# A state-space convolution with a gated top-2 feed-forward: the forward transform evicts its even part and then the full sum, the mirrored part is summed by an accumulating DMA, and the x term moves to TensorE

## The chip, the cores and the metric

The kernel runs on one core of a Trainium2 chip. The metric is device time in microseconds (us), lower is better. Engines: PE is TensorE (matmul), DVE is VectorE, ACT is ScalarE, POOL is GpSimd, and SP issues most of the DMAs. PSUM is the memory that PE writes its sums to (eight banks); SBUF holds everything else.

## The reference, cut to what matters

x is `A_u`, 2048 x 512 in bfloat16: 2048 time steps, 512 channels.

```
def _A_ref(u, A_re, A_im, B_re, B_im, C_re, C_im, log_dt, Dskip):
    dt = jnp.exp(log_dt)[:, None]
...
    P = jnp.exp(logdA[:, :, None] * l[None, None, :])
    K = jnp.einsum("dn,dnl,dn->dl", Cc, P, dB).real
...
    Yf = Uf * Kf[None, :, :, :]
    y = irfft2(Yf, (1, L2)).astype(jnp.bfloat16)[:, :, 0, :L]
    return y.transpose(0, 2, 1) + u * Dskip[None, None, :]

g = _sigmoid((x * gate_w).sum(-1, keepdims=True))
a = _A_ref(x, ...)
b = _B_ref(x, ...)    # x, plus a feed-forward's result on the 2 rows with the largest x @ w_r
return g * a + (1 - g) * b
```

So a is a causal convolution of each channel with a kernel K of 2048 taps, itself a sum over 128 complex exponentials per channel; b is x with two rows corrected; the output mixes them by a gate for each time step.

## The kernel before, in words

The program is recorded first: every step is an entry of one list (`Prog.op`), with the buffers that it reads and writes. The text `ORDER` then gives the order in which these entries stand on each engine, `SECOND` says which of two possible engines takes an entry that could run on either, and `PLACES` gives the PSUM bank or buffer of each short-lived tile (`Prog.fixed`). `Prog.emit` works out the semaphore waits. Nothing is reordered at run time: each engine takes its list from the front, and an instruction that waits holds back all that stand behind it. Costs that are written with the entries serve a planner outside the kernel.

One-line helpers record single steps, so many instructions have a helper's line: L452 `TT` (DVE tensor_tensor), L456 and L457 `TS`, L459 `STT`, L463 `AC` (an ACT activation), L465/L467 `EV` (a copy, by ACT or DVE), L469/L471 `SQ` (a square, either engine), L475/L477 `SCL` (a multiplication by a constant, either engine), L480 `DMA`.

The work, in the order of recording:

- `exps1`, `exps2` (lines about 600): powers of the exponentials, by small matmuls with scaled identities (L598, L609) and ACT exponentials.
- `routing`: transposes of x (L767), the gate and the router's scores (L782), the two rows with the largest score (L797, L801), and their feed-forward (L850, L864). The result is scattered into the output's memory, into which x has been copied, and x is reloaded from there into its buffer `U` by `reload()`.
- `tab1`, `tab2`: tables of sines and products for the two column halves h = 0, 1 of 256 channels (ACT: int32 to sine and the masks, L463, L668, L696; DVE: products).
- `forward(blk)` for the two blocks of 1024 time steps (L902): a transform to frequencies with the constants `F`, whose time steps are split into even and odd ones. For each of four frequency tiles `ft` and each of two parts (real, imaginary) 8 matmuls of 128x512 sum even and odd steps in a bank; the sum is evicted to `X` (pm = 0). Then 4 matmuls with `UO`, minus twice the odd steps, go on top, and even minus odd is evicted as the mirrored part (pm = 1). `UO` is made by one 128x2048 scaling.
- `kgen(h)` (L920): K's samples from the tables, evicted to `KA`, and picked from there by L933, L937, L946, L949 into `KC`.
- `kspec(h)` (L975): the spectrum `KK` of K, by matmuls of 128x256. Its second half starts from the first: as a carry by PE matmuls of 128x512 (L967) for the halves h listed in `CPE`, else by an ACT activation into PSUM (L962, shown under L463).
- `products(h, qds, blks)`: products of `X` and `KK` as DVE multiplications of 128x4096, for the second block with an accumulating DMA issued by POOL (L1019, 1 MB) that adds one product to another, and sums and differences of 128x1024 (all L452) that write the result over `X`.
- `inverse(h)` (L1052): the inverse transform with the constants `G` (2 MB, loaded late). Each PSUM tile is first filled with the x term, x times a factor for its time steps, by ACT (L1037, two activations of 128x256, shown under L463); a one-hot matmul (L1040) adds to the rows that the feed-forward changed; 16 matmuls of 128x256 add the transform; two evictions (L1060, ACT or DVE) multiply by the gate. Output DMAs of 128 KB follow.

What the change and the prediction's steps touch: `forward`, `products`, `inverse`, `kspec` through `CPE`, the end of `routing` (the factor of the x term), `late`, the buffers, and the orders. The factor of the x term and the gate stand in columns of a small tile:

```
TS(SG(0, 128, 64, (1, 16)), SGB(0, 128, 32, (1, 16)), 1.0e-20, ALU.max, ...)
P.op(DVE, lambda h: h.reciprocal(SG(0, 128, 80, (1, 16)), SG(0, 128, 64, (1, 16))), ...)
TT(SG(0, 128, 96, (1, 16)), SG(0, 128, 80, (1, 16)), SGB(0, 128, 48, (1, 16)), MUL, ...)
```

## Time and profile before

| what | value |
|---|---|
| runs | 154.81, 155.19, 155.6 us (median 155.19) |
| profiled execution | 155.34 us, of which the span from first to last instruction is 153.5 us |
| granted TensorE clock, mean | 0.989 |
| instructions in the span | 3887 |
| matmuls of the forward transform (L902) | 192, 44.7 us busy |
| matmuls of the inverse (L1052) | 256, 29.1 us busy |
| x term on ACT (L463, 128x256 into PSUM) | 32, 14.3 us busy |
| accumulating DMAs (L1019) | 4 of 1 MB, 7.9 to 11.6 us from issue to landing |
| DMA traffic | 26.21 MB, mean 171 GB/s |

A line of the profile names the code line, the engine, the operation, where it writes and reads (`AR` is the SBUF arena, `ps` is PSUM), and the shape. "Busy" adds the time in which such instructions ran; neighbours on one engine overlap at their edges, so a mean duration can be longer than the step from one to the next. "Idle before" is the engine's idle time just ahead of them, and what ended it. The chain of work is followed backwards from the last instruction, at each step to what released it. Most of the kernel has DVE and PE running side by side, so the chain's shares say which of the two it happened to follow, and the windows say whether the other was idle.

### The profile page before, as it was taken

Reading aid. Unit: us, or ns where it says so; the run is one execution under the profiler, and the core shown is the slowest. Engines: PE = TensorE matmul, PEld = TensorE weight load, DVE = VectorE, ACT = ScalarE, POOL = GpSimd, SP = SyncE. Lnnn points to the kernel's source line nnn. Section 1 sums busy time; section 2 is a strip of 40 time slices with the busy share of each in tenths; the row PEclk is TensorE's granted clock in tenths of the full one; section 3 lists DMA queues with packets and bytes.
Section 4 is the critical chain, followed back from the end, with each engine's and each line's share of the span. In section 5 each row is a group of like instructions: output and inputs, shape, how many; then the busy total and the mean of one; then the engine's idle time right before and its main releaser. Section 6 shows DMA issues by size and latency. Waiting matters only on the chain.

```text
span 153.5 us, 3887 instructions
## 1 busy us (share of the span) xinstructions
PE 138.1 (90%) x1661; PEld 100.0 (65%) x1661; DVE 137.3 (89%) x207; ACT 124.4 (81%) x206; POOL 9.7 (6%) x17
## 2 busy tenths in 40 slices
PE   1877999999999999999989999988866999999990
PEld 1666734665446444996447879985754888887870
DVE  0599999999999999899999999992999999999941
ACT  3399899989979999999958968576599599995530
POOL 3000000000100000014000000340000001130000
PEclk9999999995999999999999999999999999999999
DMA  4899999937700001700079200199998000799974
GB/s 138 255 341 411 409 404 398 352 102 277 275 0 4 0 0 26 242 14 1 0 190 384 114 4 0 33 184 190 229 391 345 11 2 4 136 173 188 249 214 138
DMA packets 13523, 26.21 MB, mean 171 GB/s; under 512 B 1175, under 2 KB 8098, under 8 KB 13346
## 3 DMA queue, kind: packets, MB, share of 16 engines
q1 hardware_dynamic: 11410, 21.11, 39.1%
q0 software_dynamic: 1120, 4.20, 15.6%
q10 hardware_dynamic: 976, 0.66, 1.4%
q8 instruction: 13, 0.21, 0.6%
q14 instruction: 4, 0.03, 0.1%
HBM read 19.66 MB, written 4.20 MB: 155 GB/s over the span
## 4 chain that ended last, share of the span: by engine, by line
DVE 47%; PE 36%; DMA 9%; ACT 3%; issue 3%; SPq 1%
DVE AR L452 39%; PE ps L902 18%; PE ps L1052 7%; DMA AR<-AR 7%; PE ps L920 6%; DVE AR L467 3%; PE ps L850 2%; DMA AR<-in_A_log_dt_dram 2%; DVE AR L477 2%; ACT AR L463 1%; PE ps L598 1%; DVE AR L456 1%; DVE AR L459 1%; PE ps L864 1%; DVE AR L797 1%
## 5 line engine op out<-in xcount | busy, mean ns | idle before, releaser
L452 DVE TENSOR_TENSOR AR<-AR 128x1024 bf16<-128x1024 bf16 (+10 forms) x127 | 110.6, 923 | 7.8 <-ACT AR L463 5.4
L467 ACT ACTIVATE AR<-ps 128x1024 bf16<-128x1024 f32 (+10 forms) x57 | 48.2, 865 | 14.1 <-PE ps L975 4.7
L902 PE MATMUL ps<-AR 128*128 128x512 bf16 x192 | 44.7, 388 | 0.0
L902 PEld LDWEIGHTS ps<-AR 128*128 128x128 bf16 x192 | 18.8, 101 | 21.4 <-issue 1.9
L1052 PE MATMUL ps<-AR 128*128 128x256 bf16 x256 | 29.1, 273 | 1.8 <-DMA AR<-c_inv 1.4
L1052 PEld LDWEIGHTS ps<-AR 128*128 128x128 bf16 x256 | 24.7, 98 | 5.5 <-DVE AR L452 2.7
L975 PE MATMUL ps<-AR 128*128 128x256 bf16 x160 | 19.3, 273 | 1.5 <-ACT AR L467 0.7
L463 ACT ACTIVATE AR<-AR 128x1024 bf16<-128x1024 int16 (+5 forms) x24 | 18.3, 774 | 1.7 <-DMA AR<-in_A_log_dt_dram 1.2
L975 PEld LDWEIGHTS ps<-AR 128*128 128x128 bf16 x160 | 15.3, 98 | 5.4 <-ACT AR L467 1.8
L463 ACT ACTIVATE ps<-AR 128x256 f32<-128x256 bf16 (+1 forms) x36 | 18.2, 544 | 0.1
L920 PEld LDWEIGHTS ps<-AR 128*128 128x128 bf16 x512 | 17.9, 96 | 0.7 <-ACT AR L696 0.4
L920 PE MATMUL ps<-AR 128*128 128x84 bf16 (+1 forms) x512 | 18.1, 196 | 0.0
L1060 ACT ACTIVATE AR<-ps,AR 128x256 bf16<-128x256 f32 x26 | 11.8, 478 | 5.7 <-PE ps L1052 5.6
L463 ACT ACTIVATE AR<-ps 128x512 bf16<-128x512 f32 (+1 forms) x18 | 12.1, 789 | 1.9 <-PE ps L598 1.9
L477 ACT ACTIVATE AR<-AR 128x256 int32<-128x256 f32 (+2 forms) x25 | 12.4, 528 | 0.0
L668 ACT ACTIVATE AR<-AR 128x1024 int32<-128x1024 int32 (+1 forms) x10 | 8.9, 888 | 0.1
L1019 POOL DMA_DIRECT2D AR<-AR x4 | 4.9, 1216 | 60.4 <-DVE AR L452 30.6
L477 DVE TENSOR_SCALAR AR<-AR 128x256 int32<-128x256 f32 (+3 forms) x25 | 8.4, 350 | 0.0
L767 PE MATMUL ps<-AR 128*128 128x128 bf16 x64 | 4.4, 220 | 1.8 <-DVE AR L452 1.2
L767 PEld LDWEIGHTS ps<-AR 128*128 128x128 bf16 x64 | 3.6, 98 | 2.6 <-DVE AR L452 1.4
L933 PE MATMUL ps<-AR 128*32 128x128 bf16 x64 | 4.7, 421 | 0.6 <-ACT AR L467 0.6
L609 PE MATMUL ps<-AR 128*128 128x128 bf16 x8 | 2.0, 475 | 3.1 <-DMA AR<-in_A_C_im_dram 3.1
(63 smaller groups left out, 81.8 us busy)
## 6 DMA issues: line engine op xcount, KB each, us to landing
AR<-AR POOLq DMA_DIRECT2D x4, 1024.0 KB, 9.2
AR<-c_ksp SPq DMA_DIRECT2D x5, 512.0 KB, 4.3
AR<-in_A_u_dram SPq DMA_DIRECT2D x4, 512.0 KB, 7.3
AR<-c_fwd SPq DMA_DIRECT2D x4, 512.0 KB, 10.2
AR<-out_dram SPq DMA_DIRECT2D x4, 512.0 KB, 8.2
AR<-c_inv SPq DMA_DIRECT2D x1, 2048.0 KB, 14.6
AR<-in_B_w_up_dram SPq DMA_DIRECT2D x1, 1792.0 KB, 11.6
AR<-in_B_w_gate_dram SPq DMA_DIRECT2D x1, 1792.0 KB, 17.0
```

The lines of the kernel that those rows point to most:

```text
L452: return P.op(DVE, lambda h: h.tensor_tensor(out=o, in0=a, in1=b, op=op), rd, wr, cost=cst or tt_cost(o, a, b), **k)
L463: return P.op(ACT, lambda h: h.activation(out=o, in_=a, func=func, scale=scale, bias=bias), rd, wr, cost=0.185 + nel(o) * 0.833e-3 + (0.09 ...
L467: return P.op((ACT, DVE), (lambda h: h.activation(out=o, in_=a, func=ACTF.Copy), lambda h: h.tensor_copy(o, a)), rd, wr, cost=(0.185 + n * ...
L477: return P.op((ACT, DVE), (lambda h: h.activation(out=o, in_=a, func=ACTF.Copy, scale=c), lambda h: h.tensor_scalar(out=o, in0=a, scalar1= ...
L668: P.op((DVE, ACT), (lambda hh: hh.tensor_scalar(out=w, in0=w, scalar1=16384.0, scalar2=None, op0=ALU.add), lambda hh: hh.activation(out=w, ...
L767: last = h.transpose(bb(0, 128, db * 256 + t_ * 128, (1, 128)), U(0, 128, (2 * q + t_) * D + db * 128, (1, 128)), IDN(0, (1, 128)))
L902: last = h.matmul(o, w, x, start=(pm + par + st == 0), stop=(par == 1 and st == 3), skip_group_check=(pm == 1))
L920: last = hh.matmul(pb(0, 128, g // 6 * 512 + g % 6 * W4 + o, (1, n)), TP[h][1 - i // 2](0, 128, (b0 + g) * 128, (1, 128)), r[i](0, 128, (b ...
L975: last = hh.matmul(pb(0, 128, n * 256, (1, 256)), KP[u](0, 128, tau * 128, (1, 128)), KC[h](0, 128, jg * 256, (1, 256)), start=(k == 0 and ...
L1019: P.op(POOL, lambda hh, p=p, t=t: hh.dma_start(v(p), v(t), accum_op=ADD, max_dma_last_dim=4096), qk(t, 0, 1, 2, 3), qk(p, 0, 1, 2, 3), cos ...
L1052: r = hh.matmul(pb(0, 128, e * 256, (1, 256)), G(0, 128, ((par * 2 + part) * 4 + ft) * 512 + (2 * t2 + e) * 128, (1, 128)), X(0, 128, h * ...
L1060: P.op((ACT, DVE), (lambda hh, o=o, i_=i_, g_=g_: hh.activation(out=o, in_=i_, func=ACTF.Copy, scale=g_), lambda hh, o=o, i_=i_, g_=g_: hh ...
```

## The change

The forward transform now sums the 4 matmuls of the even steps first and evicts them, multiplied by -2, to the mirrored part (pm = 1); the 4 matmuls of the odd steps go on top, and the full sum is evicted to pm = 0. `UO` and its scaling are gone, and each part takes 8 matmuls where it took 12. For every pair of frequency tiles and each block POOL issues one accumulating DMA (512 KB, four in all) that adds pm = 0 to pm = 1: odd minus even, so the last sum and difference of `products` change places.

The x term is a matmul: `late` makes 16 identities of 128x128, each multiplied by the factor of one tile of time steps (rounded to bfloat16), by ACT activations, and two matmuls of 128x256 per PSUM tile start the inverse. Seven operations of 16 elements (of which two are copies) work out the rounded factor and a gate that makes up for the rounding. `CPE` takes in h = 1, so the carry of the second spectrum is on PE. The evictions of the inverse stand two to an entry, on ACT or as one DVE tensor_tensor, except at the very end.

`X` is laid out by blocks, the feed-forward's buffers move with it, and `ORDER`, `SECOND` and `PLACES` are new. With them the first DMA on SP is log_dt, the loads of `F`, the feed-forward's weights and the smaller inputs stand in another order, three reloads of `U` instead of two stand ahead of `G` and one behind it, and ACT has four table loads instead of two. `kgen`, `tab1`, `tab2` and the rest of `kspec` compute what they did.

```diff
@@ -253,7 +253,7 @@
 NM = len(MAG2)
 ACC = ()
 DAC = ((0, 0), (0, 1), (1, 0), (1, 1))
-CPE = (0,)
+CPE = (0, 1)
 GROUPS = [[2 + 4 * i + k for k in range(4)] for i in range(4)] + [[1, 18, 19, 20]]
 KUSE = [(0, 0), (0, 1), (0, 2), (0, 3), (1, 4)]
 NU = len(KUSE)
@@ -369,29 +369,29 @@
...
@@ -496,11 +496,10 @@
-        UO = B("uo", oF + 16 * KB, 4 * KB)
-        XB = [[B("x%d%d" % (h_, k_), oX + (16 * h_ + 8 * k_) * KB, 8 * KB) for k_ in range(2)] for h_ in range(2)]
+        XB = [[B("x%d%d" % (h_, k_), oX + (16 * k_ + 8 * h_) * KB, 8 * KB) for k_ in range(2)] for h_ in range(2)]
@@ -518,8 +517,8 @@
-        XT = [B("xt%d" % i, oX + (16 * (i // 2) + 8 + 4 * (i % 2)) * KB, 4 * KB) for i in range(4)]
-        WD = [B("wd%d" % i, oX + (16 * i + 8) * KB, 8 * KB) for i in range(2)]
+        XT = [B("xt%d" % i, oX + (16 + 4 * i) * KB, 4 * KB) for i in range(4)]
+        WD = [B("wd%d" % i, oX + (16 + 8 * i) * KB, 8 * KB) for i in range(2)]
@@ -545,6 +544,7 @@
+        DX16 = B("dx16", oI + 16 * KB, 4 * KB)
@@ -791,6 +791,13 @@
+            EV(SGB(0, 128, 64, (1, 16)), SG(0, 128, 96, (1, 16)), [(SG, "x")], [(SGB, "x")])
+            EV(SG(0, 128, 0, (1, 16)), SGB(0, 128, 64, (1, 16)), [(SGB, "x")], [(SG, "xr")])
+            TT(SG(0, 128, 32, (1, 16)), SG(0, 128, 96, (1, 16)), SG(0, 128, 0, (1, 16)), SUB, [(SG, "x"), (SG, "xr")], [(SG, "d")])
+            TS(SG(0, 128, 48, (1, 16)), SG(0, 128, 0, (1, 16)), 1.0e-30, ALU.max, [(SG, "xr")], [(SG, "r")])
+            P.op(DVE, lambda h: h.reciprocal(SG(0, 128, 48, (1, 16)), SG(0, 128, 48, (1, 16))), [], [(SG, "r")], cost=0.3)
+            TT(SG(0, 128, 32, (1, 16)), SG(0, 128, 32, (1, 16)), SG(0, 128, 48, (1, 16)), MUL, [(SG, "r")], [(SG, "d")])
+            STT(SG(0, 128, 112, (1, 16)), SG(0, 128, 32, (1, 16)), 1.0, SG(0, 128, 64, (1, 16)), ADD, MUL, [(SG, "d"), (SG, "m")], [(SG, "n")])
@@ -881,29 +888,37 @@
         def late():
             P.op(POOL, lambda h: h.memset(OHR(0, 128, 0, (1, len(ERT) * 128)), 0.0), [], [OHR], cost=0.4)
             DMA([(OHR(32, NE, 0, (1, len(ERT) * 128)), oh_c[:, :])], [], [(OHR, "e")], NE * 1024)
+            for j in (1, 0):
+                def da(hh, j=j):
+                    for i in range(8 * j, 8 * j + 8):
+                        r = hh.activation(out=DX16(0, 128, i * 128, (1, 128)), in_=CB(0, 128, 0, (1, 128)), func=ACTF.Copy, scale=SG(0, 128, 0 + i, (1, 1)))
+                    return r
+                P.op((DVE, ACT), (lambda hh, j=j: hh.tensor_tensor(out=DX16(0, 128, j * 1024, (128, 8), (1, 128)), in0=CB(0, 128, 0, (0, 8), (1, 128)), in1=SGB(0, 128, 64 + 8 * j, (1, 8), (0, 128)), op=MUL), da),
+                     [CBI, (SGB, "x"), (SG, "xr")], [(DX16, j)], cost=(1.22, 2.9))
         def reload():
             for j in (1, 0):
                 for k in range(2):
                     DQ([(U(0, 128, (j * 8 + k * 4) * D, (2 * D, 2), (1, 2 * D)), dr(out, (1024 * j + 512 * k) * D, (2 * D, 128), (256 * D, 2), (1, 2 * D)))], [DX], [(U, (t, h_)) for t in range(8 * j + 4 * k, 8 * j + 4 * k + 4) for h_ in range(2)], 524288)
 
         def forward(blk):
-                SCL(UO(0, 128, 0, (1, 4 * D)), U(0, 128, (blk * 8 + 1) * D, (2 * D, 4), (1, D)), -2.0, uk(*range(blk * 8 + 1, blk * 8 + 8, 2)), [UO])
                 for ft in range(4):
                     pb = psum(2, full=True)
-                    for pm in range(2):
+                    for par in range(2):
                         for part in range(2):
-                            def fw(h, blk=blk, ft=ft, pm=pm, pb=pb, part=part):
+                            def fw(h, blk=blk, ft=ft, par=par, pb=pb, part=part):
                                 last = None
-                                o = pb(0, 128, part * 512, (1, 512))
-                                for par in range(pm, 2):
-                                    for st in range(4):
-                                        w = F[ft](0, 128, ((par * 4 + st) * 2 + part) * 128, (1, 128))
-                                        x = UO(0, 128, st * D, (1, D)) if pm else U(0, 128, (blk * 8 + st * 2 + par) * D, (1, D))
-                                        last = h.matmul(o, w, x, start=(pm + par + st == 0), stop=(par == 1 and st == 3), skip_group_check=(pm == 1))
+                                for st in range(4):
+                                    last = h.matmul(pb(0, 128, part * 512, (1, 512)), F[ft](0, 128, ((par * 4 + st) * 2 + part) * 128, (1, 128)), U(0, 128, (blk * 8 + st * 2 + par) * D, (1, D)),
+                                                    start=(par + st == 0), stop=(st == 3), skip_group_check=(par == 1))
                                 return last
-                            P.op(PE, fw, [F[ft]] + ([UO] if pm else uk(*range(blk * 8, blk * 8 + 8))), [(pb, part)], cost=(8 - 4 * pm) * 0.2157)
-                        EV(X(0, 128, blk * 4096 + ft // 2 * 1024 + pm * 512 + ft % 2 * 256, (2048, 2), (8192, 2), (1, 256)), pb(0, 128, 0, (512, 2), (256, 2), (1, 256)),
-                           [pb], [xk(hh, blk, part, pm, ft) for hh in range(2) for part in range(2)])
+                            P.op(PE, fw, [F[ft]] + uk(*range(blk * 8 + par, blk * 8 + 8, 2)), [(pb, part)], cost=4 * 0.2157)
+                        o, i_, sc = X(0, 128, blk * 8192 + ft // 2 * 1024 + (1 - par) * 512 + ft % 2 * 256, (2048, 2), (4096, 2), (1, 256)), pb(0, 128, 0, (512, 2), (256, 2), (1, 256)), (-2.0, 1.0)[par]
+                        P.op((ACT, DVE), (lambda hh, o=o, i_=i_, sc=sc: hh.activation(out=o, in_=i_, func=ACTF.Copy, scale=sc), lambda hh, o=o, i_=i_, sc=sc: hh.tensor_scalar(out=o, in0=i_, scalar1=sc, scalar2=None, op0=ALU.mult)),
+                             [pb], [xk(hh, blk, part, 1 - par, ft) for hh in range(2) for part in range(2)], cost=(0.185 + 1024 * 0.833e-3, 0.16 + 1024 * 1.04e-3))
+                    if ft % 2:
+                        xv = lambda pm: X(0, 128, blk * 8192 + ft // 2 * 1024 + pm * 512, (2048, 4), (1, 512))
+                        xs_ = lambda pm: [xk(hh, blk, part, pm, f) for hh in range(2) for part in range(2) for f in (ft - 1, ft)]
+                        P.op(POOL, lambda hh, d=xv(1), c=xv(0): hh.dma_start(d, c, accum_op=ADD), xs_(0), xs_(1), cost=1.3, nbytes=524288, dma=True, tag="acc")
 
         def kgen(h):
             r = RW[h]
@@ -1024,7 +1039,7 @@
                 for parts in (((0,), (1,)) if last(h, blk, qds[-1]) else ((0, 1),)):
                     n, p0 = len(parts), parts[0]
                     y = lambda pm: p(0, 128, (2 * p0 + pm) * W, (2 * W, n), (1, W))
-                    for pm, op in ((0, ADD), (1, SUB)):
+                    for pm, op in ((0, SUB), (1, ADD)):
                         TT(X(0, 128, xo(blk, p0, pm), (2048, n), (1, W)), y(0), y(1), op, qk(p, *parts), [xk(h, blk, part, pm, ft) for part in parts for ft in fts])
         def inverse(h):
             for blk in (1, 0):
@@ -1032,9 +1047,12 @@
                 tbs = lambda t2, par: [blk * 8 + (2 * t2 + e) * 2 + par for e in range(2)]
                 for t2 in range(2):
                     for par in range(2):
-                        pb = bufs[t2, par] = psum(seed=True)
-                        for e, tb in enumerate(tbs(t2, par)):
-                            AC(pb(0, 128, e * 256, (1, 256)), U(0, 128, tb * D + h * HC, (1, HC)), ACTF.Copy, [(SG, "x"), (U, (tb, h))], [(pb, e)], scale=SG(0, 128, 96 + tb, (1, 1)))
+                        pb = bufs[t2, par] = psum(full=True)
+                        def xt(hh, pb=pb, tbs_=tbs(t2, par)):
+                            for e, tb in enumerate(tbs_):
+                                r = hh.matmul(pb(0, 128, e * 256, (1, 256)), DX16(0, 128, tb * 128, (1, 128)), U(0, 128, tb * D + h * HC, (1, HC)), start=(e == 0), stop=False, skip_group_check=True)
+                            return r
+                        P.op(PE, xt, [(DX16, blk)] + [(U, (tb, h)) for tb in tbs(t2, par)], [pb], cost=2 * 0.1092)
                         for e, tb in enumerate(tbs(t2, par)):
                             if tb in ERT:
                                 P.op(PE, lambda hh, pb=pb, e=e, tb=tb: hh.matmul(pb(0, 128, e * 256, (1, 256)), OHR(0, 128, ERT.index(tb) * 128, (1, 128)), ZB(0, 128, h * HC, (1, HC)), start=False, stop=False, skip_group_check=True),
@@ -1050,15 +1068,22 @@
                                         for c in cs:
                                             part, ft = c % 2, 2 * q + c // 2
                                             r = hh.matmul(pb(0, 128, e * 256, (1, 256)), G(0, 128, ((par * 2 + part) * 4 + ft) * 512 + (2 * t2 + e) * 128, (1, 128)),
-                                                          X(0, 128, h * 8192 + blk * 4096 + part * 2048 + ft // 2 * 1024 + par * 512 + ft % 2 * 256, (1, 256)), start=False, stop=(q == 1 and e == 1 and c == 3), skip_group_check=True)
+                                                          X(0, 128, blk * 8192 + h * 4096 + part * 2048 + ft // 2 * 1024 + par * 512 + ft % 2 * 256, (1, 256)), start=False, stop=(q == 1 and e == 1 and c == 3), skip_group_check=True)
                                     return r
                                 P.op(PE, iv, [G] + [xk(h, blk, part, par, ft) for part in sorted({c % 2 for c in cs}) for ft in (2 * q, 2 * q + 1)], [pb.buf], cost=2 * len(cs) * 0.1092)
                             if q == 0:
                                 continue
-                            for e, tb in enumerate(tbs(t2, par)):
-                                o, i_, g_ = U(0, 128, tb * D + h * HC, (1, HC)), pb(0, 128, e * 256, (1, HC)), SG(0, 128, 64 + tb, (1, 1))
-                                P.op((ACT, DVE), (lambda hh, o=o, i_=i_, g_=g_: hh.activation(out=o, in_=i_, func=ACTF.Copy, scale=g_), lambda hh, o=o, i_=i_, g_=g_: hh.tensor_scalar(out=o, in0=i_, scalar1=g_, scalar2=None, op0=MUL)),
-                                     [pb.buf, (SG, "m")], [(U, (tb, h)), (pb.buf, "r")], cost=(0.473, 0.484))
+                            tb0 = tbs(t2, par)[0]
+                            for ee in (((0,), (1,)) if last(h, blk, q) else ((0, 1),)):
+                                def oa(hh, ee=ee, pb=pb, tb0=tb0):
+                                    for e in ee:
+                                        tb = tb0 + 2 * e
+                                        r = hh.activation(out=U(0, 128, tb * D + h * HC, (1, HC)), in_=pb(0, 128, e * 256, (1, HC)), func=ACTF.Copy, scale=SG(0, 128, 112 + tb, (1, 1)))
+                                    return r
+                                def od(hh, ee=ee, pb=pb, tb0=tb0):
+                                    e, n, tb = ee[0], len(ee), tb0 + 2 * ee[0]
+                                    return hh.tensor_tensor(out=U(0, 128, tb * D + h * HC, (2 * D, n), (1, HC)), in0=pb(0, 128, e * 256, (256, n), (1, HC)), in1=SG(0, 128, 112 + tb, (2, n), (0, HC)), op=MUL)
+                                P.op((ACT, DVE), (oa, od), [pb.buf, (SG, "n")], [(U, (tb0 + 2 * e, h)) for e in ee] + [(pb.buf, "r")], cost=((0.473, 0.484) if len(ee) == 1 else (0.88, 0.7)))
                 for st in range(4):
                     tb = blk * 8 + st * 2
                     DMA([(dr(out, (1024 * blk + 256 * st) * D + h * HC, (2 * D, 128), (D, 2), (1, HC)), U(0, 128, tb * D + h * HC, (D, 2), (1, HC)))],
```

More of the change, by code (lines that the diff above doesn't have):

```diff
@@ L389 @@
[L389 to L391 removed]
+    "000000000000000000000000000000000000100000000000000000000000000010100010101010100000100100010000000000000000000000000000010001000000000000000000000011"
@@ L769, in routing @@
                 P.op(PE, tr, uk(2 * q, 2 * q + 1) + [CBI], [bb], cost=0.455)
-                EV(XT[0](0, 128, q * 256, (8 * KB, 2), (L, 2), (1, 256)), bb(0, 128, 0, (512, 2), (256, 2), (1, 256)), [bb], [(XT[i], q) for i in range(4)])
+                EV(XT[0](0, 128, q * 256, (2 * L, 2), (L, 2), (1, 256)), bb(0, 128, 0, (512, 2), (256, 2), (1, 256)), [bb], [(XT[i], q) for i in range(4)])
             w8 = misc(True)
@@ L985, in products @@
             q0 = qds[0] * 1024
-            xo = lambda blk, part, pm: h * 8192 + blk * 4096 + part * 2048 + pm * 512 + q0
+            xo = lambda blk, part, pm: blk * 8192 + h * 4096 + part * 2048 + pm * 512 + q0
             fts = [2 * qd + e for qd in qds for e in range(2)]
```

45 lines of the change are left out of this document (22 added, 23 removed).

## The prediction

> **What bounds the kernel.** I read the busy shares first, then the chain that ended last, then the rows behind its last half, and the windows of its stages.
>
> The page, first and fourth part:
>
> ```profile
> PE 138.1 (90%) x1661; PEld 100.0 (65%) x1661; DVE 137.3 (89%) x207; ACT 124.4 (81%) x206; POOL 9.7 (6%) x17
> ...
> DVE 47%; PE 36%; DMA 9%; ACT 3%; issue 3%; SPq 1%
> ```
>
> Three engines are over 80% busy. Taking work from one of them gains only where that one is late. The chain (start, us, what) from the first product on:
>
> ```profile
> 92.74 4.48 DVE AR L452 x2
> 97.23 0.10 DVE AR L474
> 97.32 0.22 issue
> 97.54 10.16 DMA AR<-AR
> 107.70 0.02 issue
> 107.72 11.17 DVE AR L452 x14
> 118.90 0.47 issue
> 119.36 1.94 DVE AR L452 x4
> ...
> 138.71 10.83 PE ps L1052 x96
> 149.54 0.02 issue
> 149.56 0.48 ACT AR L1060
> 150.04 0.02 issue
> 150.07 0.48 DVE AR L1060
> ```
>
> From the first 4096-wide product at 92.74 a fixed sequence follows: two products, an accumulating DMA of 10.16 us, 11.17 us of DVE sums, then the inverse transform. The windows (span, then busy us and count of PE, PEld, DVE, ACT, POOL) say who limits it:
>
> ```profile
> 20.00:30.00 10.00, 9.76 (x79) 4.58 (x77) 9.90 (x31) 9.97 (x12) 0.00 (x0) 1.00 1.05 384
> 60.00:70.00 10.00, 10.00 (x235) 8.57 (x234) 9.40 (x16) 9.97 (x15) 1.32 (x2) 1.00 0.36 108
> 119.30:150.50 31.20, 29.86 (x269) 25.91 (x269) 28.64 (x35) 23.44 (x54) 2.40 (x2) 1.00 0.58 125
> ```
>
> Ahead of the products PE, DVE and ACT are all full. From the first inverse matmul (119.30) to the last (149.54) PE ran 269 matmuls in 30.24 us with 0.37 us of gaps: 0.111 us each. The end is PE-bound. The rows that the change touches (busy, mean ns, idle before):
>
> ```profile
> L902 PE MATMUL ps<-AR 128*128 128x512 bf16 x192 | 44.7, 388 | 0.0
> L463 ACT ACTIVATE ps<-AR 128x256 f32<-128x256 bf16 x32 | 14.3, 483 | 0.0
> L463 ACT ACTIVATE ps<-AR 128x1024 f32<-128x1024 bf16 x4 | 4.1, 1026 | 0.1
> ```
>
> **The sum, part by part.** It is made against the profiled execution: span 153.5 and 1.84 us around it, 155.34; the median of the runs is 155.19, so I correct nothing.
>
> *Forward transform.* 64 of 192 matmuls go. In the chain 40 of them take 8.74 us, 0.2185 each: PE is relieved of 14.0 us, nearly all between 32.7 and 74.7, where the chain is PE. But DVE and ACT are full beside it, so I ask what each needs up to the first product.
>
> DVE: two 1024-wide products less (2 x 0.60 by the chain), two 1024-wide scalings less (2 x 0.34), the 2048-wide scaling for the old -2 x odd buffer less (0.6), three 256-wide more (3 x 0.20), a 512-wide less (0.2), a reciprocal more (0.25): -1.8. The waits behind L696, L463 and L463 (0.6, 0.28, 0.31) go, since what they waited for now stands earlier: -1.2. At the start log_dt is loaded first (-0.55), but the copy of the constants no longer fills DVE's wait for PE L598 (0.85 becomes 1.95): +0.55. DVE alone could begin the first product at 92.74 - 2.4 = 90.3.
>
> PE and ACT: kernel generation (L920, 256 matmuls, 8.9 us) starts at about 59.8, when both its inputs and the first half of the forward are done, against 61.4. Then 32 forward matmuls (7.0), the extraction (about 4), four spectra of 16 at 0.111 (7.1); ACT's sixth spectrum eviction, which the second product needs, ends at about 91.2. A load of the spectrum's first constants now follows the last forward matmul (4.3 us to landing) and may add 0.5 to 0.8. So the first product starts at 91.2 to 92.4; I take 91.9, which is 0.8 earlier.
>
> *Four accumulating DMAs on POOL.* The rows have four of twice the size (L1019: issue 1.2 us, landing 7.9 to 11.6). At half the size I take 1.2 and 5. The last has its inputs by about 74 and stands behind a memset that waits for ACT at about 82; it lands near 88, while the sums that read its target come after 107. At nothing, then, with some 17 us of cover; below nothing only by the evictions, whose count is unchanged. The swapped ADD and SUB cost nothing.
>
> *Carry of the second spectrum on PE.* Four ACT seeds of 1.03 go (row above); eight 512-wide matmuls come, 1.7 us on PE, 0.44 of it behind the first inverse matmul.
>
> *x term.* 32 ACT seeds (14.3 us) go; 32 PE matmuls of 0.111 come (3.6), 8 ahead of the first inverse matmul and 24 behind it. Sixteen 128x128 activations come: nearest rows 171 ns (128x8) and 394 (128x256), so 2.7 to 6.3 us; I take 4. They stand in the 15 us while the first accumulating DMA runs, and the spectrum evictions behind them finish 3 us before DVE reads them. The seven 16-element operations (0.16 to 0.3 us each) stand in DVE's wait for that DMA (1.8 us before).
>
> *Table loads.* Two become four. Each is 1.28 us (20.47 to 21.75), and the next activation began at 21.77: +2.6. With two 1024-wide squares moved to ACT (+2.1) and one scaling and other steps off it, ACT has 3.3 us more ahead of the products. It idles there at 74.5 to 90.7 for 4.2 us in sum, which hides it if nothing DVE needs sooner is delayed. The page "ScalarE: Activation LUTs" of the Trainium skill (section "What ACT_TABLE_LOAD costs") gives 1283 ns for the load, which the row shows, and about 1380 ns for a drain on top, which the 0.02 us gap does not show; by that rule two more would be +5.3.
>
> *From the first product on.* The first accumulating DMA lands 14.9 us after it, as before (92.74 to 107.7); then DVE has two 4096-wide products moved behind that wait (2 x 2.24), nine 1024-wide steps (9 x 0.56) and 0.6 of small ones: 10.1. First inverse matmul at 91.9 + 25.0 = 116.9, against 119.30. The inverse constants, then waited for (landing 14.6 us after issue at 104.55), are issued a little sooner with one reload less ahead; about 116.5, a near tie.
>
> *The end.* From there PE has 256 + 24 + 8 one-hot + 4 spectrum matmuls, 292 x 0.111, and 0.44 of carry: 32.85 us against 30.24. Last matmul 149.75; two evictions 0.95 and the output DMA 2.95 as before: span 153.7, with the 1.84 around it 155.5. A span up to 154.2 (first product at 92.4) gives 156.0. I take **155.8**: the 2.4 us that the first half gains are paid back by PE's 2.6 us at the end, where ACT's relief is worth nothing. DVE's last sum, at 146.4 before, comes 2.5 us earlier and is not the end either.
>
> **The rivals.**
>
> *Faster, 153.2.* The first accumulating DMA took 10.16 us while others shared the queues; the shortest took 7.9. If it gets that, DVE's wait shrinks by 2.3 us, and with the first product at 91.2 or sooner the inverse can start 2.6 us earlier than in the forecast, if its constants are in by 114.3. For it: one reload less, and 391 GB/s in the slices where they came. Against: they came just when needed before.
>
> *Slower, 158.4.* ACT takes the bound: between 10 and 70 us it idles under 0.9 in 10, and the sines that DVE multiplies come through it. If the two loads delay the tables, DVE waits 2.6 us and the first product starts at 94.5. It decides when kernel generation's inputs come later than about 60.5. By the Trainium skill's drain rule, named above, another 2.7 would follow: 161.1; the 0.02 us gap speaks against it.
>
> *POOL's DMAs are late, 158.* The sums of the first half need the halved target; if an accumulating DMA waits while DVE is busy, all that follows slides by some 2.2 us (12.4 instead of 10.2 to landing). The four rows of L1019 speak against it: issues of 1.19 to 1.26 us beside a DVE busy 10 of 10. The Trainium skill's page "SBUF — State Buffer" (section "SBUF: two separate sides") says that POOL cannot write descriptors while DVE runs a two-port mode; the rows show no such stall.
>
> *The change does not do what it says:* the counts of the order do show 128 forward matmuls and no seeds, so I give it nothing.
>
> **How the numbers follow.** Forecast (154.9 to 156.6) 0.38; faster 0.28 (151.8 to 154.4); slower by ACT 0.26 (156.6 to 160); the drain rule 0.03; late POOL DMAs 0.05. No change means within 0.5%, about what a measurement of this kernel can tell: 154.4 to 156.0. Of the forecast 0.22 fall inside and 0.16 above. So faster 0.28, same 0.22, slower 0.50. The range reaches into both neighbours and leaves about 0.05 below and 0.12 above: 152.4 to 159.0; the forecast's own range stands above.
>
> **What would show it.** PE busy in the forward windows (32 to 75) well under 10 of 10. First 4096-wide product at 91 to 92.5; at 94 or later ACT was the bound, with DVE waiting for ACT before 60. First accumulating DMA of the products some 10 us to landing. First inverse matmul near 117, 292 matmuls at 0.111 without gaps behind it; gaps there, waiting for DVE or for the evictions, would break the sum. The wait for the constants at most 1 us. The forecast is wrong if the last 33 us are not PE's, or if the first product has moved by more than 1.5 us.

## The result, and the profile after

The changed kernel took 160.23 us (median of 4 runs, 158.72 to 161.08) beside 155.15 for the kernel before on the same chip: ratio 1.0315, 95% interval 1.022 to 1.041. The forecast was 155.8, the range 152.4 to 159.0. The profiled execution took 159.48 us with a span of 157.7. Medians here and below take in every run, while the ratios leave out runs of a slower state (over 1.5% above the fastest of the same kernel), in which a profiled execution can fall too.

The page of after, first and fourth part:

```profile
PE 132.1 (84%) x1629; PEld 99.1 (63%) x1637; DVE 136.4 (86%) x209; ACT 115.9 (74%) x191; POOL 26.5 (17%) x21
...
DVE 51%; PE 32%; DMA 12%; issue 2%; ACT 1%; SPq 0%; DVEq 0%
```

PE has 6.0 us less than before and ACT 8.5, and yet the span grew by 4.2. DMA went from 9% to 12% of the chain. Its end (start, us, what):

```profile
90.04 8.74 DVE AR L452 x4
98.88 0.20 issue
99.08 16.23 DMA AR<-AR
115.34 3.70 DVE AR L452 x6
119.04 0.10 DVE AR L459
119.16 0.42 DVE AR L452
119.61 0.70 DVE AR L452
120.36 3.02 PE ps L1070 x16
...
152.19 1.76 PE ps L1070 x16
153.97 0.48 ACT AR L1081
154.48 0.47 ACT AR L1081
```

The DMA here is another one than before. Before, the chain went through the first accumulating DMA of the products (10.16 us). Now that one, issued at 94.68, lands 8.1 us later, at 102.8, and the chain goes through the second: issued at 99.08, landed at 115.3, 16.2 us. DVE stands idle for it (waits of DVE: total, times, longest), and PE behind DVE:

```profile
DVE AR L452 <- DMA AR<-AR: 7.4, 2, 6.6
```

Three groups of after (busy, mean ns, idle before):

```profile
L911 PE MATMUL ps<-AR 128*128 128x512 bf16 x123 | 32.2, 419 | 1.4 <-ACT AR L467 0.9 <-issue 0.5
L1053 PE MATMUL ps<-AR 128*128 128x256 bf16 x32 | 6.0, 281 | 6.0 <-DVE AR L452 6.0
L894 ACT ACTIVATE AR<-AR 128x128 bf16<-128x128 bf16 x16 | 4.8, 387 | 0.0
```

L911 is the forward transform (5 of its 128 records are missing), L1053 the x term on PE with the 6.0 us wait ahead of it, and L894 the scaled identities. The windows (span, then busy us and count of PE, PEld, DVE, ACT, POOL, then the granted clock):

```profile
20.00:30.00 10.00, 5.62 (x14) 2.25 (x15) 10.00 (x29) 9.95 (x16) 0.31 (x1) 0.51 1.06 380
60.00:70.00 10.00, 9.15 (x216) 8.00 (x215) 9.89 (x16) 9.54 (x15) 3.66 (x3) 1.00 0.83 143
110.00:120.00 10.00, 4.00 (x34) 2.88 (x31) 4.60 (x9) 3.56 (x4) 0.00 (x0) 0.79 0.50 152
120.00:130.00 10.00, 9.83 (x78) 7.95 (x78) 10.00 (x9) 1.86 (x3) 1.19 (x1) 0.87 0.17 31
```

From 110 to 120 every engine is less than half busy: this hole is the loss. The inverse constants landed at 115.5 (14.3 us after 101.19), so without DVE's wait PE would have waited for them instead: of the 6.6 us some 4.9 count (120.36 less 115.5). Early on DVE and ACT are as full as before, and PE has got room at half its clock.

What stands beside the second accumulating DMA? The DMA queues of after from 104 to 108 (packets, MB, share of 16 engines; q0 is POOL's, q1 is SP's):

```profile
q1 hardware_dynamic: 58, 0.92, 64.6%
q0 software_dynamic: 61, 0.25, 35.7%
```

and of before from 107 to 111, when its second accumulating DMA (issued at 102.0) was under way:

```profile
q0 software_dynamic: 158, 0.65, 85.2%
q1 hardware_dynamic: 155, 0.32, 23.2%
```

Both times one packet of SP goes for one of POOL. But in after SP's packet has 16 KB (0.92 MB in 58), a row of the inverse constants, and holds an engine 0.71 us (64.6% of 4 us on 16 engines, by 58); in before it has 2 KB, a piece of the reload of `U`, and holds it 0.10 us. POOL's has 4 KB and takes 0.37. So POOL moved 0.25 MB in 4 us instead of 0.65. In both kernels three reloads of `U` stand ahead of the constants on SP and one behind them, other than I had put it under "The change"; but before issued the third at 104.12, just ahead of the constants (104.55), and after with the first two, from 75.36 on, long ahead of the constants (101.19). That is my theory P: packet turns, and no small packets left beside the second accumulating DMA. It agrees with the Trainium skill's page "DMA: Bandwidth & Descriptors" (section "Queues, rings and completion order"), by which each DMA engine goes round the queues packet by packet; the page's packet is some 9 to 17 descriptors, and whether the profile counts these or single ones no run here shows.

### The profile page after: what moved, and what is told of

The parts are those of the page before. It is cut to its first block, busy times and chain, and to the rows that moved or that the text cites. A ratio compares the mean times of both kernels' runs of the same rounds, so it can differ in the third digit from the quotient of the medians.

```text
span 157.7 us, 3820 instructions
## 1 busy us (share of the span) xinstructions
PE 132.1 (84%) x1629; PEld 99.1 (63%) x1637; DVE 136.4 (86%) x209; ACT 115.9 (74%) x191; POOL 26.5 (17%) x21
## 3 DMA queue, kind: packets, MB, share of 16 engines
q1 hardware_dynamic: 11410, 21.11, 38.9%
## 4 chain that ended last, share of the span: by engine, by line
DVE 51%; PE 32%; DMA 12%; issue 2%; ACT 1%; SPq 0%; DVEq 0%
DVE AR L452 40%; PE ps L1070 19%; DMA AR<-AR 10%; PE ps L911 5%; DVE AR L467 3%; DVE AR L477 3%; PE ps L857 2%; PE ps L1053 2%; DVE AR L456 1%; DMA AR<-c_bf 1%; PE ps L598 1%; PE ps L836 1%; DVE AR L457 1%; PE ps L871 1%; DVE AR L459 1%
## 5 line engine op out<-in xcount | busy, mean ns | idle before, releaser
L452 DVE TENSOR_TENSOR AR<-AR 128x1024 bf16<-128x1024 bf16 (+8 forms) x129 | 111.1, 912 | 11.3 <-DMA AR<-AR 7.4
L467 ACT ACTIVATE AR<-ps 128x1024 bf16<-128x1024 f32 (+10 forms) x39 | 30.5, 817 | 14.6 <-PE ps L990 11.4
L911 PE MATMUL ps<-AR 128*128 128x512 bf16 x123 | 32.2, 419 | 1.4 <-ACT AR L467 0.9
L1070 PE MATMUL ps<-AR 128*128 128x256 bf16 x256 | 31.3, 279 | 0.1
L1070 PEld LDWEIGHTS ps<-AR 128*128 128x128 bf16 x256 | 25.5, 100 | 4.0 <-DVE AR L452 0.6
L911 PEld LDWEIGHTS ps<-AR 128*128 128x128 bf16 x128 | 13.3, 107 | 17.7 <-issue 4.7
L990 PE MATMUL ps<-AR 128*128 128x256 bf16 x160 | 19.3, 273 | 0.0
L935 PEld LDWEIGHTS ps<-AR 128*128 128x128 bf16 x512 | 17.7, 96 | 0.7 <-ACT AR L916 0.6
L990 PEld LDWEIGHTS ps<-AR 128*128 128x128 bf16 x160 | 15.4, 98 | 3.9 <-ACT AR L477 0.3
L916 ACT ACTIVATE AR<-ps 128x1024 bf16<-128x1024 f32 x16 | 15.9, 1013 | 0.1
L882 POOL DMA_INDIRECT out_dram<-AR x1 | 13.5, 13480 | 12.5 <-DVE AR L456 12.5
L1034 POOL DMA_DIRECT2D AR<-AR x4 | 4.8, 1195 | 42.5 <-DVE AR L452 39.3
L1053 PE MATMUL ps<-AR 128*128 128x256 bf16 x32 | 6.0, 281 | 6.0 <-DVE AR L452 6.0
L921 POOL DMA_DIRECT2D AR<-AR x4 | 5.8, 1453 | 14.4 <-ACT AR L916 14.4
L668 ACT ACTIVATE AR<-AR 128x1024 int32<-128x1024 int32 (+1 forms) x9 | 7.7, 860 | 0.0
L477 DVE TENSOR_SCALAR AR<-AR 128x256 int32<-128x256 f32 (+2 forms) x24 | 7.7, 335 | 0.0
L1053 PEld LDWEIGHTS ps<-AR 128*128 128x128 bf16 x32 | 3.0, 99 | 6.9 <-DVE AR L452 6.3
## 6 DMA issues: line engine op xcount, KB each, us to landing
AR<-c_inv SPq DMA_DIRECT2D x1, 2048.0 KB, 14.3
```

The costliest lines, as they stand in the source:

```text
L452: return P.op(DVE, lambda h: h.tensor_tensor(out=o, in0=a, in1=b, op=op), rd, wr, cost=cst or tt_cost(o, a, b), **k)
L467: return P.op((ACT, DVE), (lambda h: h.activation(out=o, in_=a, func=ACTF.Copy), lambda h: h.tensor_copy(o, a)), rd, wr, cost=(0.185 + n * ...
L477: return P.op((ACT, DVE), (lambda h: h.activation(out=o, in_=a, func=ACTF.Copy, scale=c), lambda h: h.tensor_scalar(out=o, in0=a, scalar1= ...
L882: P.op(POOL, lambda h: h.indirect_dma_start(dr(out, 0, (D, L), (1, D)), bass.IndirectOffsetOnAxis(ap=IDX(0, 2, 0, (1, 1)), axis=0), ZB(0, ...
L911: last = h.matmul(pb(0, 128, part * 512, (1, 512)), F[ft](0, 128, ((par * 4 + st) * 2 + part) * 128, (1, 128)), U(0, 128, (blk * 8 + st * ...
L916: P.op((ACT, DVE), (lambda hh, o=o, i_=i_, sc=sc: hh.activation(out=o, in_=i_, func=ACTF.Copy, scale=sc), lambda hh, o=o, i_=i_, sc=sc: hh ...
```

## The experiments

Each was timed with the kernel before on the same chip; where a ratio is given, its 95% interval is in brackets. The first product came anywhere from 90.0 to 97.1 us in the profiled executions, for reasons ahead of most of these edits, so the last column gives the time from it to the end of the span; before has 60.8 there. P stands against S (POOL's DMA is held up by a busy DVE) and B (only the sum of the bytes counts).

| run | edit | median us | ratio | first product to end, us |
|---|---|---|---|---|
| after | | 160.23 | 1.0315 (1.022 to 1.041) | 67.7 |
| e1 | constants in small packets | 155.53 | 1.0013 (0.995 to 1.007) | 62.4 |
| e2 | reload ahead of the constants | 158.51 | 1.0231 (1.012 to 1.034) | 64.2 |
| e3 | second sum on DVE | 157.53 | 1.0162 (1.004 to 1.028) | 64.6 |
| e4 | before, constants ahead of the reload | 161.24 | 1.031 (1.015 to 1.047) | 66.0 |
| e5 | e1, x term on ACT | 161.86 | none | 67.2 |
| e6 | e1, PE kept busy early | 154.78 | 0.9997 (0.994 to 1.006) | 61.8 |
| e7 | e1, forward's DMAs small | 155.44 | 0.9971 (0.990 to 1.004) | 62.1 |
| e8 | e5, constants issued sooner | 168.32 | none | 74.5 |
| e9 | constants in 4 KB packets | 160.96 | 1.0294 (1.017 to 1.042) | 65.3 |
| e10 | e1 without the x term | 156.18 | 1.001 (0.995 to 1.007) | 62.9 |
| e11 | e3, DVE's order changed | 157.6 | 1.0092 (1.003 to 1.015) | 64.5 |
| e12 | constants behind the second sum | 159.65 | 1.0278 (1.018 to 1.038) | 67.0 |

For e5 and e8 no ratio can be given; the median of before, beside them, was 155.71. The intervals of e2, e3, e4, e9 and e12 lie above 1, but reach to both sides of a loss of 2%.

**e1: the constants in small packets.**

```diff
-DMA([(G(0, 128, 0, (1, 8192)), g_c[:, :])], [], [G], 2097152)
+P.op(SP, lambda h: [h.dma_start(G(0, 128, 0, (1, 8192)), g_c[:, :], max_dma_last_dim=1024)], ...)
```

> After, with one edit: the load of the inverse constants (2 MB, c_inv) is cut into 2 KB packets instead of rows of 16 KB. Theory P (packets): the DMA engines take a packet of each queue in turn, so against 16 KB packets the second accumulating DMA, with 4 KB packets, got a fifth of the bytes and landed 16.2 us after its issue; with 2 KB packets it lands 8 to 10.5 us after issue, DVE's wait of 6.6 us goes, the first inverse matmul moves from 120.4 to 116-117 (the constants then last), time 155.5 us (154.5 to 157). Rival S (POOL's DMA is held up by a busy DVE): landing stays near 16, time near 160. Rival B (only the sum of the bytes counts): landing stays at 13 to 16, time 158 to 160.

The packets came out at 1 KB, not 2. From e1's timeline, DVE behind its wait for the second accumulating DMA (in brackets the idle time and what ended it):

```profile
112.72 3.70 DVE L452 TENSOR_TENSOR AR<-AR 128x1024 bf16<-128x1024 bf16 x6 [0.79 <-DMA AR<-AR]
```

and PE at the first inverse matmul:

```profile
118.38 1.91 PE L1070 MATMUL ps<-AR 128*128 128x256 bf16 x16 [0.98 <-DMA AR<-c_inv]
```

11.1 us to landing instead of 16.2 (I had expected 8 to 10.5), DVE's wait 0.8 instead of 6.6, the constants last by 1 us, 155.53. From 106 to 108 the two queues moved 83 packets each: one for one again, but SP's now held an engine 0.06 us. S and B are out: same bytes, same DVE, and the loss is gone. What remains of the change is worth less than 0.7% either way.

**e2: the old order of the two loads on SP, in the new kernel; e4: the new order, in the kernel before.**

```diff
 # e2, SP of after                          # e4, SP of before
-c_oh, G, reload of U                       -c_oh, reload of U, G, reload of U
+c_oh, reload of U, G                       +c_oh, G, reload of U, reload of U
```

> After, with the last 512 KB reload (2 KB packets) put ahead of the load of the inverse constants on SP, where before had it. P: the second accumulating DMA shares with small packets first and lands 9 to 12 us after issue; the constants land 1.5 to 2.5 us later than in after (about 117.5) and become the last wait; time 157.0 (156 to 158.5). S: no change, about 160. B: no change in the landing of the accumulating DMA, the constants later: 160 to 162.

> Before, with the inverse constants put ahead of the 512 KB reload on SP, where after has them. P: the second accumulating DMA lands 14.5 to 17 us after issue instead of 11.6, DVE waits 3 to 4 us for it at about 113.9, time 157.5 (156.5 to 159). S and B: no change or a gain, 154 to 155.5, since the constants, for which PE waited 1.4 us, come sooner.

In e2 the landing fell to 11.5 us, as expected, and the time to 158.51, a little more than the 156 to 158.5 expected; its interval overlaps that of after, so the time alone does not show the gain. In its trace DVE also waited 2.5 us for the fourth accumulating DMA (10.8 us to landing, 9.1 in e1), and PE 1.5 us behind it; so it did in other runs, below. In e4 the kernel before got the same loss: 161.24. The second accumulating DMA in its chain:

```profile
106.38 16.55 DMA AR<-AR
```

DVE behind it, in its timeline:

```profile
122.95 5.51 DVE L452 TENSOR_TENSOR AR<-AR 128x1024 bf16<-128x1024 bf16 x9 [5.83 <-DMA AR<-AR]
```

and its queues from 112 to 116:

```profile
q1 hardware_dynamic: 66, 1.08, 70.8%
q0 software_dynamic: 64, 0.26, 32.7%
```

16.5 us to landing, a wait of 5.8, the same one-for-one packets, and PE waited 4.1 us for DVE behind it. In this execution the first product was already 4.4 us late (97.12 against 92.74), ahead of the two loads; but from there to the end it took 66.0 us against 60.8 before. By the ratio, 1.031, this is a loss as large as that of the change, made by exchanging two loads in a kernel that has nothing else of it. The wait is longer than the 3 to 4 us that I expected, and so is the time.

**e3: no second DMA; e11: the same with a better order on DVE.**

```diff
-DAC = ((0, 0), (0, 1), (1, 0), (1, 1))
+DAC = ((0, 0), (1, 0), (1, 1))
 # e11, DVE: the added 4096-wide sum first, in the wait for the first DMA;
 # two products and a sum of block 0 behind the sum that the inverse starts with
```

> After, with the second accumulating DMA (the one that landed late) replaced by a DVE addition of 128x4096, 2.26 us, at the same place of the order. P, S and B alike: no DMA of POOL left to wait for but the first; the first inverse matmul at about 116.2, the constants in at about 112; PE's 33 us behind it: time 155.2 (154.2 to 156.2). If something else than that DMA held DVE at 109 to 115, the time stays near 160. If PE is not what sets the end, the 2.26 us of DVE work show at the end and it is 157 or more.

> e3 (second sum added by DVE, no DMA to wait for) with two moves in DVE's order: that addition stands in the wait for the first accumulating DMA, and two 4096-wide products and one sum of the other block stand behind the sum that the first inverse matmul needs. The first inverse matmul moves from 118.1 to 113 to 114, when the constants land; DVE's sums for the second half then set the end: ratio 0.980 to 0.992, 152.5 to 154.5 us. If the accumulating DMAs of the second half set it, they move with DVE's order by 2 to 3 us, the same. If nothing moves, 1.016 as e3.

Both missed; in e3 its last condition came true (157 or more "If PE is not what sets the end"). In e3 the first inverse matmul came at 118.08, 2.3 us before after's, but then PE had to wait again. The chain of e3 further on:

```profile
129.54 10.85 DMA AR<-AR
140.39 0.02 issue
140.41 1.30 DVE AR L452 x2
```

That is the fourth accumulating DMA. In e11 the inverse began at 114.15, and its last matmul still ended 60.3 us behind the first product (e1: 58.4): DVE carries 2.26 us more work in a stretch that it fills. In e2, e3, e9, e10 and e11 the fourth DMA took 10.4 to 10.9 us to landing and DVE waited 2.1 to 2.6 us for it; in after, e1, e5, e6, e7 and e8 it took 8.7 to 9.5. Why is not shown.

**e10: without the x term.** In place of the two matmuls one of a single column opens the bank; the output lacks the x term.

```diff
-for e, tb in enumerate(tbs_): r = hh.matmul(pb(0, 128, e * 256, (1, 256)), DX16(...), U(..., (1, HC)), start=(e == 0), ...)
+if e == 0: r = hh.matmul(pb(0, 128, 0, (1, 1)), DX16(...), U(..., (1, 1)), start=True, ...)
```

> e1 with the x term left out: in place of its two matmuls of 128x256 each tile gets one of a single column, which opens the bank. It prices the x term on PE, which the prediction put at 24 x 0.111 = 2.7 us of the end. If PE sets the end, the stretch from the first to the last inverse matmul falls from 32.5 to 29.8 to 30.8 us (DVE's last sum, at 146.5 in e1, may keep some of it) and the ratio to before is 0.980 to 0.990 against e1's 1.001. If something else sets the end (DVE's sums, the accumulating DMAs), nothing is gained, 0.995 to 1.005.

Nothing was gained. The chain of e10 shows why:

```profile
125.54 1.19 POOL AR L1034
...
130.54 10.36 DMA AR<-AR
140.90 0.02 issue
140.93 1.30 DVE AR L452 x2
...
143.00 3.67 PE ps L1071 x32
```

With 24 matmuls less on PE (2.7 us by the prediction's price), PE waited 2.3 us in three places for DVE. From DVE's restart behind the second DMA to the last matmul it took 38.9 us here (114.07 to 152.93), 38.1 in e1 and 38.6 in after. PE's stretch is full, but a second chain beside it is as long: DVE's sums, the third and fourth accumulating DMA, and DVE's last sums. In this execution the fourth took 1.3 us longer than in e1, so the lengths agree only to about that.

**e5: the x term back on ACT (24 of 32); e8: also the constants sooner.**

```diff
-P.op(PE, xt, [(DX16, blk)] + ..., [pb])
+P.op(PE if (h, blk) == (0, 1) else ACT, xt if (h, blk) == (0, 1) else xa, ..., [pb])
 # xa: two activations of 128x256 into the bank.  e8, SP: G, c_oh, reload of U
```

> The constants in 2 KB packets as in e1, and the x term of 12 of the 16 tiles of the inverse (24 of 32 matmuls, all but the first tiles) put back on ACT at the same places of the order. Theory: PE sets the end, so the stretch from the first inverse matmul to the last falls from 32.5 us by up to 24 x 0.111 = 2.7; DVE's last sum (146.5 in e1) then comes near the end and may leave 1.5 to 2.7 of it: ratio to before 0.982 to 0.992 (e1: 1.001), about 153.5 us. Rival: ACT's seeds wait for banks and hold PE up, no gain or slower, 155.5 to 157.

> e5 with the load of the inverse constants also put ahead of the small c_oh load on SP, for which POOL's queue is waited for: issued about 3 us sooner (100.7 instead of 103.7), landing about 115.5, so that DVE at 117 is the last to let the first inverse matmul start instead of 118.4. Theory: another 0.5 to 1.3 us off e5, ratio 0.975 to 0.988. If the earlier constants slow the second accumulating DMA again, no gain over e5.

The rival held in e5: a seed on ACT can start only when a bank has been evicted, and PE waits for it (waits of PE: total, times, longest):

```profile
PE ps L1075 <- ACT ps L1058: 2.6, 1, 2.6
PE ps L1063 <- ACT ps L1058: 1.9, 1, 1.9
```

161.86 us. So in this order the x term on PE has no cost that e10 can tell (1.001 beside e1's 1.0013), and on ACT it has one. In e8 the constants, now issued beside the second accumulating DMA (100.09 and 99.93) instead of 2 us behind it, delayed it again, small packets or not (landing 15.5 us, DVE's wait 5.3), as the last sentence of its expectation had allowed; but it came out slower than e5, not the same. The queues of e8 from 104 to 108:

```profile
q1 hardware_dynamic: 1023, 1.05, 86.1%
q0 software_dynamic: 40, 0.15, 19.0%
```

and from 108 to 112:

```profile
q0 software_dynamic: 173, 0.71, 88.6%
q1 hardware_dynamic: 175, 0.18, 16.3%
```

The first is not one for one, the second is. From 105 to 106 POOL's queue moved no packet at all, while SP's moved 317; the first accumulating DMA had landed at 104.5, and the second began only near 107. So packet turns explain the stretch in which both queues moved packets, and not those 2.5 us; whether POOL's queue had nothing ready then or got no turn stays open.

**e9: 4 KB packets; e12: 16 KB packets, but behind the second sum.**

```diff
 # e9
-max_dma_last_dim=1024
+max_dma_last_dim=4096
 # e12, SP: c_oh, reload of U, G; and before the orders are fixed
+P.ops[445].deps.add(455)
```

> As e1, but the inverse constants in 4 KB packets (e1's were measured as 1 KB, after's are 16 KB). Turn-taking with the packet times of the traces: a packet of the accumulating DMA holds an engine 0.38 us, a 16 KB packet 0.71, a 1 KB packet 0.05. The second accumulating DMA has 16 packets on each of 16 engines: 16 x (0.38 + 0.71) = 17 us against 16 KB packets (after took 12.2 from the landing of the first, part of it alone), 16 x (0.38 + about 0.18) = 9 us against 4 KB. So it ends 8 to 9.5 us after the first one has landed, between e1's 6.5 and after's 12.2, and the time is 156 to 158. If only the order of the queues counts and not the size of a packet, it is after's 160.

> After, with its 16 KB packets, but the load of the inverse constants made to wait until the second accumulating DMA has landed; the reload stands ahead of it. The accumulating DMA then lands 9 to 11 us after its issue (e2 had 11.5 with the reload beside it), the constants are issued near 110 and, alone, land 7 to 9 us later, near 118: first inverse matmul 118 to 119, time 155.5 to 157.5. If 16 KB packets are slow in themselves, they land after 122 and the time is 160 or more.

The packets of e9 from 108 to 112:

```profile
q0 software_dynamic: 127, 0.52, 67.6%
q1 hardware_dynamic: 129, 0.50, 33.3%
```

One for one again, and the DMA ended 8.4 us after the first one's (107.92 to 116.30), as the packet times had said (8 to 9.5). The time, 160.96, did not come out at 156 to 158: DVE also waited 2.6 us for the fourth DMA, and in this execution the first product came 4.4 us later than in after; from there to the end it took 65.3 us, 2.4 less than after. So 1 KB packets bring the whole time back (e1) and 4 KB ones do not; packet turns account for the landing of the second DMA in both, and not for the rest of e9's time. In e12 the second DMA came in at 111.2, and the constants, alone, took 8.3 us from 111.19 to 119.5. PE in e12:

```profile
119.60 3.19 PE L1070 MATMUL ps<-AR 128*128 128x256 bf16 x16 [3.72 <-DVE AR L452]
```

The wait is put down to DVE, but DVE's sum was done at 116.1; it was the constants. PE came out of it slow: 3.19 us for 16 matmuls that take 1.75 elsewhere. The first inverse matmul, at 119.6, was 0.6 us later than I expected, the time 2 us above.

**e6: PE kept busy from 16 to 25 us; e7: the forward's accumulating DMAs cut to 8 columns** (the mirrored part is left unsummed).

```diff
 # e6: 5, 7 and 15 matmuls ahead of L782 and of the first two L808 on PE
+P.op(PE, lambda h, ...: [h.matmul(wb(0, 128, 0, (1, 512)), CB(0, 128, 0, (1, 128)), CB(0, 128, 0, (0, 4), (1, 128)), ...) for i_ in range(n_)][-1], ...)
 # e7
-xv = lambda pm: X(0, 128, blk * 8192 + ft // 2 * 1024 + pm * 512, (2048, 4), (1, 512))
+xv = lambda pm: X(0, 128, blk * 8192 + ft // 2 * 1024 + pm * 512, (2048, 4), (1, 8))
```

> e1 with 27 matmuls of 128x512 on constants, that nobody reads, in PE's three gaps between 16 and 25 us. Theory C (clock): the granted clock falls to 0.5 there because PE is idle for half of the time, and the forward and feed-forward matmuls behind run at half speed to 36 us; with the gaps filled the clock stays at 0.9 or more in that stretch and the first product comes up to 2 us sooner: ratio 0.988 to 1.0 against before. Rival: the clock costs nothing, since DVE sets that stage: clock up, ratio as e1 (1.001). Third: the clock stays at 0.5 whatever PE does, and the filling costs 1 to 3 us: 1.008 to 1.02.

> e1 with the forward's four accumulating DMAs cut from 512 columns per row to 8, so that the mirrored part is left unsummed. My theory: they land well ahead of their readers and cost nothing: ratio as e1, 0.996 to 1.006. Rival: they hold up reloads, spectrum constants or the products' own accumulating DMA: 1.5 to 3 us faster, ratio 0.98 to 0.99.

The window of e6:

```profile
20.00:30.00 10.00, 8.84 (x40) 3.79 (x37) 9.49 (x25) 9.97 (x17) 0.31 (x1) 0.83 1.06 378
```

The clock there rose to 0.83 from 0.56 in e1 (0.51 in after), less than the 0.9 expected, and the time stayed (0.9997 beside e1's 1.0013): that fits DVE and ACT, 9.5 and 10.0 us busy, setting that stage. In e7 the time stayed too: the four DMAs of the forward cost nothing that can be told, as forecast.

## Why the prediction was wrong

The step that failed is in "From the first product on": "The first accumulating DMA lands 14.9 us after it, as before (92.74 to 107.7); then DVE has two 4096-wide products moved behind that wait (2 x 2.24), nine 1024-wide steps (9 x 0.56) and 0.6 of small ones: 10.1." Seven of those nine steps come after the second accumulating DMA has landed, since the first of the seven reads it, and I costed that one at nothing. Before, it was hidden: 11.6 us to landing, at 113.6, behind DVE work that began at 107.7. After, the same DMA took 16.2, and DVE stood idle for it for 6.6 us. I had seen its cause and used it for one thing only: "one reload less ahead" made the constants come sooner, and I did not ask whom the reload had protected.

By terms, forecast against the profiled execution:

- First product: 91.9 against 90.04. DVE alone could begin "at 92.74 - 2.4 = 90.3": that sum was right, and in this execution nothing else was late. PE's and ACT's path, which I took for the later one at 91.2 to 92.4, did not hold DVE up, and the miss is more than the 1.5 us that the prediction names as a sign of being wrong, to the good. In other executions something was late, below.
- Four accumulating DMAs of the forward: 5 us to landing against 6.2 to 9.8, the last in at 90.6 instead of 88; their readers come later, and e7 shows no cost.
- First accumulating DMA of the products: landing 14.9 us after the first product against 12.7; the faster rival's condition (7.9 to landing) nearly held with 8.1.
- From the first product to the first inverse matmul: 25.0 against 30.3, of which the unforeseen wait is 6.58. DVE went on 13.0 us after the first product instead of 14.9, which gave back 1.9, and its steps took 10.7 instead of 10.1.
- The end on PE: 32.85 against 33.6. Its first 16 matmuls took 3.02 us instead of 1.75, behind 6 us in which PE was idle; the rest is 0.5 shorter than forecast.
- "The end is PE-bound": half right. PE is full there, but e10 shows DVE's sums and the fourth accumulating DMA to be as long, so the 2.6 us that I charged PE for the x term would not have come back without it.

With the one wait gone the sum comes out: e1 took 155.53, the forecast was 155.8, and its profiled execution had the first product at 92.4, the first inverse matmul 25.9 us later and 32.5 us on PE from there. Part of this is luck: the 92.4, near my 91.9, comes from an execution in which PE stood still for 1.4 us early on (the last section), and not by the path that I had added up; without such a stop the first product came at 90.0 to 92.0. That the first half's gain is paid back at the end holds, but for the wait; that the x term on PE is what pays it back does not, by e10.

The rivals: "Slower by ACT" did not come; no wait of DVE for ACT shows ahead of 60, and two more table loads (1283 ns each) were hidden. "POOL's DMAs are late" named the right place and the wrong reason (a busy DVE, 2.2 us); L1034's four issues took 1.19 to 1.20 us beside it, and e1 and e4 show that the transfer was slow, not the issue. "Faster" had both of its early conditions, and the constants at 115.5 instead of 114.3; the second DMA forbade it.

## What to carry to other kernels

Where an order of DMAs changes, list for each transfer in flight what now runs beside it and with which packet size: a reload of small packets ahead of a large load can be the cover of a third transfer on another queue. A transfer that nobody waits for has a slack, the time from its landing to its first reader; for each one behind the changed place, compare that slack with how much later it may now land, and do not put it at nothing because it cost nothing before. A full engine at the end of a chain is not yet the bound: look for a second chain of the same length before its work is given a price.

## What the runs showed of the hardware that I had not expected

*A late packet of the instruction queue.* In 7 of the 12 profiled executions of the new kernel's first half PE stood still for 1.4 to 2.4 us inside a group of matmuls that wait for no semaphore, as in e5:

```profile
33.74 2.85 PE L857 MATMUL ps<-AR 128*128 128x2 bf16 x101 [0.27 <-ACT AR L467]
39.02 0.46 PE L857 MATMUL ps<-AR 128*128 128x2 bf16 x11 [2.43 <-issue]
```

In all seven a 16 KB packet of the instruction queue moved between 36 and 39 us, among other transfers at 380 to 402 GB/s; in the five without the wait it had come before 36. With the wait the first product came at 92.4 to 94.3, without it at 90.0 to 92.0. That the packet is the cause was not tried.

*A slow scatter on POOL.* The scatter's indirect DMA in the timeline of after:

```profile
47.50 13.48 POOL L882 DMA_INDIRECT out_dram<-AR  x1 [12.52 <-DVE AR L456]
```

and in that of before:

```profile
68.99 1.95 POOL L875 DMA_INDIRECT out_dram<-AR  x1 [0.22 <-issue]
```

13.5 us in place of 1.95, beside ten DVE products without a gap (47.16 to 57.98). But before had DVE at work without a gap too, on products and scalings from 65.8 to 72.1, so a busy DVE alone does not tell the two rows apart, and the cause stays open. By the Trainium skill's page "SBUF — State Buffer" (section "SBUF: two separate sides") POOL cannot write descriptors while DVE runs a two-port mode; no stall of that kind shows in the row of before, nor in the products' accumulating DMAs (issues of 1.19 to 1.20 us). It cost nothing: the reloads that wait for it are issued only at 75.3 and read at 110.

*The clock.* PE, idle for 6 us, came back slow: 0.189 us a matmul instead of 0.109, at a granted clock of 0.62 from 120.3 to 123.4 and of 1.00 behind it. The Trainium skill's "TensorE: Matmul & The Clock Gate" (section "What's actually happening") has the clock throttled after idle time; these rows agree, and so does e6, where the clock rose when the gaps were filled.
